# Batch 0 of a pooled-attention and feed-forward kernel: v in two loads, half its values with tokens in rows, w_in in other pieces, and batch 1 loaded as q, k, q

## The chip, the cores and the metric

The kernel runs on one core of a Trainium2 chip. The metric is the time of one execution in microseconds (us) of device time, the median of several runs. The engines are named as in the profile: PE (TensorE), DVE (VectorE), ACT (ScalarE), POOL (GpSimd) and SP (SyncE). PEld is TensorE's loading of weights.

## What is computed

Attention over pooled keys and values, and then a feed-forward layer with the gate h cos(h):

```python
k_p = k.reshape(B, H, 72, 8, 64).mean(axis=3)      # B = 8, H = 8, S = 576, D = 64
v_p = v.reshape(B, H, 72, 8, 64).mean(axis=3)
attn = softmax(q @ k_p.transpose(0, 1, 3, 2) / 8)
x = (attn @ v_p).transpose(0, 2, 1, 3).reshape(4608, 512)
h = x @ w_in                                       # 512 x 2048
out = (h * cos(h)) @ w_out                         # 2048 x 512
```

All inputs and the output are float32 in HBM. The kernel computes in bfloat16; the loads that GpSimd issues convert on the way.

## The kernel before

The 4608 tokens are cut into nine tiles of 512 (the loop over t). A tile has an up stage (x @ w_in, then cosine and product into g_sb) and a down stage (g_sb @ w_out, stored). Attention of batch b = t + 1 is fitted between the down matmuls of tile t, so batch 0's attention stands ahead of the loop and batch 1's first part (its pooling of k and the transposes of q) stands in the up stage of tile 0. From tile 1 on the down product uses seven products of half size instead of eight (down_products); tile 0 uses plain matmuls (down_mm). There is no scheduler: every engine runs its instructions in the order in which the code issues them, and that order is written out by hand.

The work is placed as follows.

- Batch 0 has four units (BY_HEADS): heads 0 to 3 with tokens 0 to 255 and 256 to 511, then heads 4 to 7 with the same tokens. For each unit there are score matmuls (`scores`, L234), an exponential on ScalarE (L241), column sums by a matmul with ones, whose inverse is taken as exp(-ln) on ScalarE (`sums_first`, L313, L317, L318), and values (`values_then`, L327), which VectorE multiplies by the inverse into xT (L329). xT holds x transposed: features in partitions, in four chunks of 128 (ki), tokens in columns. Heads 0 to 3 fill chunks 0 and 1, heads 4 to 7 chunks 2 and 3.
- v is pooled by TensorE (`pool_v_mm`, L186, head pairs j0 to j1) and copied to vz by VectorE (L188); k likewise (`pool_k_mm`, L178, copied to kk at L151). q is transposed by TensorE against an identity (`q_transpose_mm`, L215, copied at L216).
- `values_rows` (L288 to L305), used from batch 2 on, puts the tokens in rows: 8 matmuls per unit with the exponentials as weights (L296), a reciprocal (L299), one multiply (L301), and a transposing DMA into xT.
- `up_mm` (L354) issues the up matmuls of pair fp (two chunks of 128 of the 2048 hidden features), for ki from k0 to k1. `up_bank` names the PSUM bank: tile 0 takes banks 0, 2, 1 in turn. Before the loop, pairs 0 and 1 are issued for ki 0 and 1 only (L559, L560). `up_g` follows with cosine (L364) and product (L368).
- In the up stage of tile 0, the pooling of batch 1's k stands behind pair 4, and the transposes of its q behind pairs 5 and 6 (L573 to L580). The down stage of tile 0 takes w_out pieces 0, 2, 1, 3 in that order (L601), and `fill` (L617) places the attention of batch 1 between its matmuls.

Loads with conversion are issued by GpSimd in this order (L488 to L523): q heads 0 to 3 of batch 0, k heads 4 to 7, q heads 4 to 7, v; w_in pieces 0, 1 and 2 (512 columns each, all four ki chunks); k of batch 1, the first half of its q, w_in piece 3, the second half of its q; w_out piece 0, v of batch 1, and w_out pieces 2, 1 and 3. The first half of k of batch 0 comes on SyncE's queue. Some matmuls without use (`warm_up`, L528) stand ahead and between.

Of the kernel before, what the change touches and what calls it, by code (L numbers as in the profile page):

```python
# [10 lines left out]
BF16 = mybir.dt.bfloat16  # L11
# [9 lines left out]
def kernel(  # L21
# [9 lines left out]
    nc = tc.nc  # L31
# [28 lines left out]
    msb = ctx.enter_context(tc.tile_pool(name="msb", bufs=3))  # L60
    psum = ctx.enter_context(tc.tile_pool(name="psum", bufs=1, space=bass.MemoryType.PSUM))

    w_in_sb = [wpool.tile([128, KCH, 512], BF16, name=f"w_in_sb{i}") for i in range(4)]
    w_out_sb = [wpool.tile([128, 4, d_model], BF16, name=f"w_out_sb{i}") for i in range(4)]
    xT = wpool.tile([128, KCH, n_tokens], BF16, name="xT")
    g_sb = wpool.tile([128, FFCH, TILE], BF16, name="g_sb")
# [28 lines left out]
    def load_even(dst, b, src, j0=0, j1=KCH):  # L95
        nc.gpsimd.dma_start(out=dst[:, j0:j1].rearrange("p j t d -> p j (t d)"), in_=even_view(src, b, j0, j1))  # L96
# [23 lines left out]
        q_tile(b)  # L120
        load_even(staged["q", b], b, q)

    def load_w_in(cg):
        nc.gpsimd.dma_start(  # L124
            out=w_in_sb[cg],
            in_=moe_w_in[:, cg * 512:(cg + 1) * 512].rearrange("(k p) f -> p k f", p=128))


    def load_w_out(cg):
# [52 lines left out]
    def pool_v_mm(b, pair, j0=0, j1=KCH):  # L182
        vb = staged["v", b]
        for t in range(ROW):
            for hp, rows in enumerate(half):
                nc.tensor.matmul(pair[:Sp, hp, 0:(j1 - j0) * D], lhsT=groups[rows, t, :], rhs=vb[rows, j0:j1, t, :],  # L186
                                 start=(t == 0), stop=(t == ROW - 1))
        nc.vector.tensor_copy(out=v_part(b)[:, j0:j1].rearrange("p j a d -> p a j d"),  # L188
                              in_=pair[:Sp, :, 0:(j1 - j0) * D].rearrange("p a (j d) -> p a j d", d=D))
# [28 lines left out]
    def ex_col(u, i):  # L218

        (c0, n), (h0, nh) = u  # L220
        return (i // 2 % 2 * (nh // 2) + i // 4 * 2 + i % 2) * n

    def scores(b, u, pair):
        scores_mm(b, u, pair)
        scores_exp(b, u, pair)
# [59 lines left out]
        else:  # L285
            later.append(mul)

    def values_rows(b, u, pair):  # L288

        (c0, n), (h0, nh) = u  # L290
        ex = att.pop(("ex", b, u))
        ps = pair.rearrange("p b n -> p (b n)").rearrange("p (j w) -> p j w", w=2 * 128)
        for i in range(nh):
            pj, hp = divmod(i, 2)
            v_and_sum = vz[b % 2].rearrange("p j a d -> p j (a d)")[:, pj, hp * (3 * D - 1):hp * (3 * D - 1) + D + 1]
            nc.tensor.matmul(ps[0:n, pj, hp * (D + 1):(hp + 1) * (D + 1)], lhsT=ex[:, ex_col(u, i):ex_col(u, i) + n],  # L296
                             rhs=v_and_sum)
        inv = asb.tile([128, KCH, 2], FP32, name="inv_rows", tag="inv_rows", bufs=2)
        nc.vector.reciprocal(out=inv[0:n], in_=ps[0:n, :, D:D + 2])  # L299
        x = asb.tile([128, d_model], BF16, name="x_rows", tag="x_rows", bufs=4)  # L300
        nc.vector.tensor_tensor(  # L301
            out=x[0:n].rearrange("p (j a d) -> p j a d", j=KCH, a=2),
            in0=ps[0:n, :, 0:2 * (D + 2)].rearrange("p j (a w) -> p j a w", a=2)[:, :, :, 0:D],
            in1=inv[0:n].unsqueeze(3).to_broadcast([n, KCH, 2, D]), op=mybir.AluOpType.mult)
        nc.sync.dma_start_transpose(out=xT[:, :, b * S + c0:b * S + c0 + n], in_=x[0:n])  # L305

    def sums_first(b, u, cs):

        (c0, n), (h0, nh) = u
        ex = att["ex", b, u]  # L310
        for i in range(nh):
            hp = i % 2
            nc.tensor.matmul(cs[hp * 64:hp * 64 + 64, (i // 2) * n:(i // 2 + 1) * n], lhsT=ones[:Sp, :],  # L313
                             rhs=ex[:, ex_col(u, i):ex_col(u, i) + n])
        w = nh * n // 2
        inv = inverse_tile(w)
        nc.scalar.activation(out=inv, in_=cs[:, 0:w], func=ACTF.Ln)  # L317
        nc.scalar.activation(out=inv, in_=inv, func=ACTF.Exp, scale=-1.0)  # L318
        att["inv", b, u] = inv

    def values_then(b, u, ao):

        (c0, n), (h0, nh) = u
        ex = att.pop(("ex", b, u))
        for i in range(nh):
            pj, hp = divmod(h0 + i, 2)
            nc.tensor.matmul(ao[hp * 64:hp * 64 + 64, (i // 2) * n:(i // 2 + 1) * n],  # L327
                             lhsT=vz[b % 2][:, pj, 3 * hp, :], rhs=ex[:, ex_col(u, i):ex_col(u, i) + n])
        nc.vector.tensor_mul(out=x_out(b, u, slice(0, 128)), in0=cols(ao, u), in1=cols(att.pop(("inv", b, u)), u))  # L329
# [4 lines left out]
    def sin_tables():  # L334
        nc.scalar.preload_act_table_set("trig_and_small")
# [6 lines left out]
    def up_bank(t, fp):  # L342
        i = list(up_order(t)).index(fp)
        if t < FIRST:
            return (banks[0], banks[2], banks[1])[i % 3]
        return (banks[0], banks[2], banks[1], obanks)[i % 4 if i < 7 else 0]

    def up_mm(t, fp, k0=0, k1=KCH):

        h = up_bank(t, fp)  # L350
        for j in range(2):
            fc = 2 * fp + j
            for ki in range(k0, k1):
                nc.tensor.matmul(h[j] if h is obanks else h[:, j, :], lhsT=w_in_sb[fc // 4][:, ki, fc % 4:512:4],  # L354
                                 rhs=xT[:, ki, t * TILE:(t + 1) * TILE],
                                 start=(ki == 0), stop=(ki == KCH - 1))

# [130 lines left out]
    load_even(staged["q", 0], 0, q, 0, 2)  # L488
    load_even(staged["k", 0], 0, k, 2, 4)
    load_even(staged["q", 0], 0, q, 2, 4)  # L490
    load_even(staged["v", 0], 0, v)
    identity = consts.tile([128, 128], BF16, name="identity")
    make_identity(nc, identity)
    dist, sign = [x.rearrange("p f n -> p (f n)").bitcast(FP32)[:, 0:ROW * Sp].rearrange("p (t n) -> p t n", t=ROW)
# [13 lines left out]

    kv_even_tiles(1)
    q_tile(1)  # L510
    for cg in range(3):
        load_w_in(cg)
    load_even(staged["k", 1], 1, k)
    load_even(staged["q", 1], 1, q, 0, 2)
    load_w_in(3)
    load_even(staged["q", 1], 1, q, 2, 4)
    load_w_out(0)
    load_even(staged["v", 1], 1, v)
# [6 lines left out]
    def warm_up(n, bank):  # L525

        for i in range(n):
            nc.tensor.matmul(bank, lhsT=warm[:, 0:128], rhs=warm)  # L528
# [16 lines left out]
    for put in (q_transpose_mm(0, banks[2][:, 0, :], 9, 14), q_transpose_mm(0, obanks[0], 14, 18)):  # L545
        put(vec)
    sums_first(0, us[1], obanks[1])
    warm_up(2, banks[1][:, 0, :])
    scores(0, us[2], banks[0])
    scores(0, us[3], banks[2])  # L550
    pool_v_mm(0, banks[1], 0, 2)
    sums_first(0, us[2], banks[0][:, 0, :])
    values_then(0, us[0], obanks[1])
    pool_v_mm(0, banks[1], 2, 4)
    values_then(0, us[1], obanks[0])
    sums_first(0, us[3], banks[2][:, 0, :])
    values_then(0, us[2], obanks[1])
    values_then(0, us[3], banks[1][:, 0, :])
    up_mm(0, 0, 0, 2)  # L559
    up_mm(0, 1, 0, 2)  # L560
    sin_tables()

    for t in range(NT):
        b = t + 1
# [4 lines left out]
        for n, fp in enumerate(up_order(t)):  # L569
            up_mm(t, fp, 2 if n < 2 else 0)  # L570
            between = ()
            if t == 0:
                if fp == 4:  # L573
                    puts = pool_k_mm(1, obanks[0], 0, 2), pool_k_mm(1, obanks[1], 2, 4)
                elif fp in (5, 6):
                    g0 = 9 * (fp - 5)
                    puts = q_transpose_mm(1, obanks[0], g0, g0 + 5), q_transpose_mm(1, obanks[1], g0 + 5, g0 + 9)
                if fp in (4, 5, 6):
                    puts[0](vec)
                    between = ((puts[1], act),)  # L580
            up_g(t, fp, between)

            late = {5: (1,), 6: (3,)} if t == 1 else {4: (1, 2), 5: (3,)}
            sums = {} if t == 0 else late if b < B else {3: (1, 2), 4: (3,), 5: (4,)}
            put_gs(*[(i, 0) for i in sums.get(n, ())])
            if 0 < t and b < B:
                if n == 0:
                    q_transpose(b)
                    k_transpose(b)
                elif n == 2:  # L590
                    pool_rest(b, "v")
                    if b + 1 < B:
                        nc.gpsimd.tensor_copy(out=gate, in_=kk[b % 2][0:1, H - 1, 0:1])
                        load_q(b + 1)
                        load_kv(b + 1, "v", v)
            if n == 2:
                while stores:
                    stores.pop(0)()
# [16 lines left out]
            exp_tables()  # L615
            fill = [(1, lambda: scores(t, REST, banks[2])), (16, lambda: values(t, REST, banks[1]))]
        if t == 0:  # L617
            fill = [(2, lambda: scores(t, REST, banks[1])), (2, S_(0, 0)), (8, lambda: pool_v_mm(1, banks[2])),
                    (8, lambda: values(t, REST, banks[1])),
                    (8, lambda: put_weights(0, nc.vector, (3, 2))), (8, S_(1, 0)), (8, V_(0, 2)),  # L620
                    (18, S_(2, 1)), (18, lambda: put_weights(0, nc.vector, (4,))),
                    (18, lambda: put_weights(1, nc.vector, (1,))), (21, V_(1, 0, later)), (26, S_(3, 2)), (32, lambda: later.pop()()),
                    (32, V_(2, 1)), (40, V_(3, 0))]
        if t == FIRST:
            early_inverses.clear()
        if t < FIRST:
# [128 lines left out]
```

## Time and profile before

| what | value |
|---|---|
| median of 5 runs | 285.02 us (284.65 to 285.28) |
| profiled execution, its own time | 285.02 us |
| its span | 283.2 us |
| mean granted TensorE clock | 0.996 |
| TensorE busy | 275.3 us, 97% |
| VectorE, ScalarE, GpSimd busy | 213.0, 167.4 and 132.7 us |
| read from HBM, written | 36.70 MB, 9.44 MB |
| first up matmul of tile 0 | 16.75 us |
| first down matmul of tile 0 | 33.01 us |
| first up matmul of tile 1 | 53.03 us |

Times in the profile count from the start of the span. An instruction group is given by line, engine, operation, written and read tile, and count; a wait by who waited for whom. Matmuls are pipelined: a row of one shows its latency, so that its duration (379 ns for 128 x 512) is longer than the distance to the next one, and the distances are read from the starts in the timeline. The column of DMA share is the mean busy share of 16 engines, and can be over 1 where packets overlap.

### The profile page before, as it was taken

What the parts mean: (1) busy time and instruction counts of PE and PEld (TensorE: products, weight loads), DVE (VectorE), ACT (ScalarE), POOL (GpSimd) and SP (SyncE); (2) the same over time, 40 slices, a digit from 0 to 9 for tenths busy, and PEclk for the clock granted to TensorE, in tenths of its full rate; (3) what the DMA queues carried; (4) which work ended last, traced back from release to release, by engine and by line L of the source; (5) the groups of instructions that cost most, each with busy time, mean ns of one, the idle gap of its engine ahead of it and who ended that gap; (6) DMA issues with size and microseconds to landing.
All of it is one profiled execution on the core that took longest, in us unless ns stands there. A gap on an engine that the chain in (4) does not pass through costs nothing.

```text
span 283.2 us, 5887 instructions
## 1 busy us (share of the span) xinstructions
PE 275.3 (97%) x2378; PEld 185.2 (65%) x2378; DVE 213.0 (75%) x313; ACT 167.4 (59%) x199; POOL 132.7 (47%) x146
## 2 busy tenths in 40 slices
PE   7899999999999999999999999999999999999994
PEld 3555554456875687568756975688558855885683
DVE  6458768989947995699568966896689669846972
ACT  3886798368357735774567556655666555436600
POOL 8542114996599259924993389539910000000000
PEclk9999999999999999999999999999999999999998
DMA  7999999794839798997678959882660370015015
GB/s 158 194 207 210 214 204 217 130 189 65 147 48 172 126 213 136 138 178 145 107 142 144 191 80 169 147 175 52 125 148 3 58 148 19 2 27 121 2 37 112
DMA packets 56202, 36.13 MB, mean 128 GB/s; under 512 B 35440, under 2 KB 51312, under 8 KB 56176
## 3 DMA queue, kind: packets, MB, share of 16 engines
q0 software_dynamic: 18208, 18.07, 40.5%
q1 hardware_dynamic: 37328, 17.18, 29.6%
q10 hardware_dynamic: 640, 0.52, 0.8%
q8 instruction: 18, 0.29, 0.4%
q14 instruction: 8, 0.07, 0.1%
HBM read 36.70 MB, written 9.44 MB: 163 GB/s over the span
## 4 chain that ended last, share of the span: by engine, by line
PE 84%; DMA 12%; POOL 2%; issue 0%; DVE 0%; POOLq 0%
PE bank L354 34%; PE obank L432 33%; DMA w_out_sb<-in_moe_w_out_dram 7%; DMA w_in_sb<-in_moe_w_in_dram 5%; PE obank L354 5%; PE obank L371 4%; PE bank L234 3%; PE bank L296 2%; PE bank L432 2%; PE bank L269 1%; POOL q_b L96 1%; POOL w_in_sb L124 1%; POOL kv_st L96 0%; DVE o_two L448 0%; POOL identity masks.py:199 0%
## 5 line engine op out<-in xcount | busy, mean ns | idle before, releaser
L354 PE MATMUL bank<-xT,w_in_sb 128*128 128x512 bf16 x512 | 113.8, 379 | 0.1
L364 ACT ACTIVATE cos<-bank,half_pi 128x1024 f32<-128x1024 f32 x64 | 70.4, 1115 | 56.7 <-PE bank L354 55.9
L354 PEld LDWEIGHTS <-w_in_sb 128*128 128x128 bf16 x576 | 64.9, 113 | 57.3 <-issue 0.3
L368 DVE TENSOR_TENSOR g_sb<-bank,cos 128x1024 bf16<-128x1024 f32 x64 | 76.9, 1219 | 30.7 <-ACT cos L364 30.6
L157 POOL TENSOR_TENSOR half_sums<-kv_st 72x512 f32<-72x512 bf16 x48 | 54.3, 1158 | 9.1 <-DMA kv_st<-in_k_dram 8.6
L241 ACT ACTIVATE ex<-bank 72x1024 bf16<-72x1024 f32 (+1 forms) x40 | 35.0, 930 | 30.1 <-PE bank L234 30.0
L432 PEld LDWEIGHTS <-g 128*128 128x128 bf16 x512 | 47.8, 98 | 5.7
L432 PE MATMUL obank<-w,g 128*128 128x256 bf16 x368 | 42.6, 272 | 0.0
L432 PEld LDWEIGHTS <-g_sb 128*128 128x128 bf16 x384 | 37.0, 98 | 6.4
L163 POOL TENSOR_TENSOR half_sums<-half_sums 72x512 f32<-72x512 f32 x24 | 30.0, 1270 | 0.0
L432 PE MATMUL obank<-w_out_sb,g_sb 128*128 128x256 bf16 x240 | 28.9, 273 | 0.0
L398 DVE TENSOR_TENSOR g<-g_sb 128x1024 bf16<-128x1024 bf16 x32 | 21.9, 684 | 0.3
L719 POOL COPY gate<-g 1x1 bf16<-1x1 bf16 x5 | 0.9, 179 | 37.5 <-DVE inv_rows L299 37.5
L280 DVE TENSOR_TENSOR xT<-bank,inv 64x256 bf16<-64x256 f32 x14 | 5.9, 422 | 15.2 <-ACT inv L276 15.1
L301 DVE TENSOR_TENSOR x_rows<-bank,inv_rows 128x512 bf16<-128x512 f32 x24 | 16.6, 692 | 0.8
L432 PE MATMUL obank<-w_out_sb,g 128*128 128x256 bf16 x112 | 15.6, 273 | 0.0
L371 PE MATMUL obank<-w_out_sb,g_sb 128*128 128x512 bf16 x64 | 15.3, 379 | 0.3 <-DMA w_out_sb<-in_moe_w_out_dram 0.3
L432 PE MATMUL obank<-w,g_sb 128*128 128x256 bf16 x128 | 15.3, 273 | 0.0
L354 PE MATMUL obank<-xT,w_in_sb 128*128 128x512 bf16 x64 | 15.1, 379 | 0.0
L234 PE MATMUL bank<-qT,kk 64*72 64x128 bf16 (+2 forms) x288 | 12.1, 221 | 0.3 <-DVE qT L216 0.3
L332 ACT ACT_TABLE_LOAD x9 | 11.5, 1283 | 0.9 <-PEq L739 0.7
L234 PEld LDWEIGHTS <-kk 64*72 64x72 bf16 x288 | 8.7, 110 | 5.1 <-issue 3.4
(99 smaller groups left out, 270.0 us busy)
## 6 DMA issues: line engine op xcount, KB each, us to landing
out_dram<-o_two SPq DMA_DIRECT2D x64, 128.0 KB, 2.4
kv_st<-in_v_dram POOLq DMA_DIRECT2D x8, 576.0 KB, 12.3
kv_st<-in_k_dram POOLq DMA_DIRECT2D x7, 576.0 KB, 8.0
q_b<-in_q_dram POOLq DMA_DIRECT2D x6, 576.0 KB, 7.8
w_in_sb<-in_moe_w_in_dram POOLq DMA_DIRECT2D x4, 512.0 KB, 13.7
w_out_sb<-in_moe_w_out_dram POOLq DMA_DIRECT2D x4, 512.0 KB, 18.6
q_b<-in_q_dram POOLq DMA_DIRECT2D x4, 288.0 KB, 12.3
g_sb<-in_k_dram SPq DMA_DIRECT2D x1, 576.0 KB, 3.5
```

Of the source, the lines that this page charges most:

```text
L157: nc.gpsimd.tensor_tensor(out=s[:, h:h + 2], in0=x[:, h:h + 2, 0:4, :], in1=x[:, h:h + 2, 4:8, :], op=ADD)
L163: add(out=s[:, h:h + 4, 0:2, :], in0=s[:, h:h + 4, 0:2, :], in1=s[:, h:h + 4, 2:4, :], op=ADD)
L234: nc.tensor.matmul(pair[:Sp, bank, c:c + n].rearrange("p (g n) -> p g n", n=64), lhsT=kk[b % 2][half[r], key_slot(b, h0 + i, r), 0:Sp], rh ...
L241: nc.scalar.activation(out=ex[:, 0:nh * n].rearrange("p (a n) -> p a n", a=2), in_=pair[:Sp, :, 0:nh * n // 2], func=ACTF.Exp, scale=scale ...
L301: nc.vector.tensor_tensor(out=x[0:n].rearrange("p (j a d) -> p j a d", j=KCH, a=2), in0=ps[0:n, :, 0:2 * (D + 2)].rearrange("p j (a w) -> ...
L332: nc.scalar.preload_act_table_set("natural_log_exp_and_others")
L354: nc.tensor.matmul(h[j] if h is obanks else h[:, j, :], lhsT=w_in_sb[fc // 4][:, ki, fc % 4:512:4], rhs=xT[:, ki, t * TILE:(t + 1) * TILE] ...
L364: nc.scalar.activation(out=c, in_=ps, func=ACTF.Sin, bias=half_pi[:, :1])
L368: nc.vector.tensor_mul(out=o, in0=ps, in1=c)
L371: nc.tensor.matmul(o, lhsT=g_sb[:, fc, ms * 128:(ms + 1) * 128], rhs=w_out_sb[fc // 4][:, fc % 4, :], start=(fc == 0), stop=(fc == FFCH - 1))
L398: nc.vector.tensor_tensor(out=out[:, f0:f1], in0=x, in1=y, op=op)
L432: mms.append(lambda bank=bank, first=first, g=g, w=w, fc=fc, p=p: nc.tensor.matmul(bank[p], lhsT=g(fc, p), rhs=w(fc), start=(first and fc ...
```

## The change

- v of batch 0 comes in two loads, head pairs 0 and 1 and then 2 and 3.
- w_in comes in five pieces (WIN): rows 0 to 255 and rows 256 to 511 of the first 512 columns, all rows of the next 512, and rows 0 to 255 and 256 to 511 of the last 1024. All five are issued ahead of batch 1's loads, which follow as first half of q, k, second half of q.
- Batch 0's units 2 and 3 (heads 4 to 7) get their values with tokens in rows (`value_rows`, split off from `values_rows` and widened to units of 256 tokens and 4 heads), and TensorE transposes them back (`x_transpose_mm`); ScalarE copies the first into xT, VectorE the second. Their sums and inverses go.
- The order before the loop: pooling of v's first half ahead of the scores of units 2 and 3 (in the place of two warm-up matmuls), its second half behind the values of units 0 and 1. The two transposes stand between the first up matmuls, and the table of the sine is loaded ahead of those.
- In the up stage of tile 0, q's transposes stand behind pairs 4 and 6 and the pooling of k behind pair 5. The PSUM banks of tile 0's up stage are 1, 0, 2 in turn, and `fill` uses the banks accordingly.

```diff
@@ -60,7 +60,9 @@
     msb = ctx.enter_context(tc.tile_pool(name="msb", bufs=3))
     psum = ctx.enter_context(tc.tile_pool(name="psum", bufs=1, space=bass.MemoryType.PSUM))
 
-    w_in_sb = [wpool.tile([128, KCH, 512], BF16, name=f"w_in_sb{i}") for i in range(4)]
+
+    WIN = ((0, 512, 0, 2), (0, 512, 2, 4), (512, 512, 0, 4), (1024, 1024, 0, 2), (1024, 1024, 2, 4))
+    w_in_sb = [wpool.tile([128, k1 - k0, n], BF16, name=f"w_in_sb{i}") for i, (_, n, k0, k1) in enumerate(WIN)]
     w_out_sb = [wpool.tile([128, 4, d_model], BF16, name=f"w_out_sb{i}") for i in range(4)]
     xT = wpool.tile([128, KCH, n_tokens], BF16, name="xT")
     g_sb = wpool.tile([128, FFCH, TILE], BF16, name="g_sb")
@@ -120,10 +122,18 @@
         q_tile(b)
         load_even(staged["q", b], b, q)
 
-    def load_w_in(cg):
+    def load_w_in(i):
+        f0, n, k0, k1 = WIN[i]
         nc.gpsimd.dma_start(
-            out=w_in_sb[cg],
-            in_=moe_w_in[:, cg * 512:(cg + 1) * 512].rearrange("(k p) f -> p k f", p=128))
+            out=w_in_sb[i],
+            in_=moe_w_in[k0 * 128:k1 * 128, f0:f0 + n].rearrange("(k p) f -> p k f", p=128))
+
+    def w_in_part(fc, ki):
+
+        for w, (f0, n, k0, k1) in zip(w_in_sb, WIN):
+            f = fc // 4 * 512 - f0
+            if 0 <= f < n and k0 <= ki < k1:
+                return w[:, ki - k0, f + fc % 4:f + 512:4]
 
 
     def load_w_out(cg):
@@ -285,24 +295,40 @@
         else:
             later.append(mul)
 
-    def values_rows(b, u, pair):
+    def value_rows(b, u, pair):
 
         (c0, n), (h0, nh) = u
+        m = min(n, 128)
         ex = att.pop(("ex", b, u))
         ps = pair.rearrange("p b n -> p (b n)").rearrange("p (j w) -> p j w", w=2 * 128)
-        for i in range(nh):
-            pj, hp = divmod(i, 2)
-            v_and_sum = vz[b % 2].rearrange("p j a d -> p j (a d)")[:, pj, hp * (3 * D - 1):hp * (3 * D - 1) + D + 1]
-            nc.tensor.matmul(ps[0:n, pj, hp * (D + 1):(hp + 1) * (D + 1)], lhsT=ex[:, ex_col(u, i):ex_col(u, i) + n],
-                             rhs=v_and_sum)
+        for c in range(n // m):
+            for i in range(nh):
+                pj, hp = divmod(h0 + i, 2)
+                v_and_sum = vz[b % 2].rearrange("p j a d -> p j (a d)")[:, pj, hp * (3 * D - 1):hp * (3 * D - 1) + D + 1]
+                e0 = ex_col(u, i) + c * m
+                nc.tensor.matmul(ps[0:m, c * nh // 2 + i // 2, hp * (D + 1):(hp + 1) * (D + 1)],
+                                 lhsT=ex[:, e0:e0 + m], rhs=v_and_sum)
         inv = asb.tile([128, KCH, 2], FP32, name="inv_rows", tag="inv_rows", bufs=2)
-        nc.vector.reciprocal(out=inv[0:n], in_=ps[0:n, :, D:D + 2])
+        nc.vector.reciprocal(out=inv[0:m], in_=ps[0:m, :, D:D + 2])
         x = asb.tile([128, d_model], BF16, name="x_rows", tag="x_rows", bufs=4)
         nc.vector.tensor_tensor(
-            out=x[0:n].rearrange("p (j a d) -> p j a d", j=KCH, a=2),
-            in0=ps[0:n, :, 0:2 * (D + 2)].rearrange("p j (a w) -> p j a w", a=2)[:, :, :, 0:D],
-            in1=inv[0:n].unsqueeze(3).to_broadcast([n, KCH, 2, D]), op=mybir.AluOpType.mult)
-        nc.sync.dma_start_transpose(out=xT[:, :, b * S + c0:b * S + c0 + n], in_=x[0:n])
+            out=x[0:m].rearrange("p (j a d) -> p j a d", j=KCH, a=2),
+            in0=ps[0:m, :, 0:2 * (D + 2)].rearrange("p j (a w) -> p j a w", a=2)[:, :, :, 0:D],
+            in1=inv[0:m].unsqueeze(3).to_broadcast([m, KCH, 2, D]), op=mybir.AluOpType.mult)
+        return x[0:m]
+
+    def values_rows(b, u, pair):
+        (c0, n), _ = u
+        nc.sync.dma_start_transpose(out=xT[:, :, b * S + c0:b * S + c0 + n], in_=value_rows(b, u, pair))
+
+    def x_transpose_mm(b, u, x, bank):
+
+        ps = bank.bitcast(BF16)[:, 0:512].rearrange("p (j n) -> p j n", j=2)
+        for c in range(2):
+            for j in range(2):
+                nc.tensor.matmul(ps[:, j, c * 128:(c + 1) * 128], x[:, (2 * c + j) * 128:(2 * c + j + 1) * 128],
+                                 identity, is_transpose=True)
+        return lambda copy: copy(out=x_out(b, u, slice(0, 128)), in_=ps)
 
     def sums_first(b, u, cs):
 
@@ -342,16 +368,16 @@
     def up_bank(t, fp):
         i = list(up_order(t)).index(fp)
         if t < FIRST:
-            return (banks[0], banks[2], banks[1])[i % 3]
+            return (banks[1], banks[0], banks[2])[i % 3]
         return (banks[0], banks[2], banks[1], obanks)[i % 4 if i < 7 else 0]
 
-    def up_mm(t, fp, k0=0, k1=KCH):
+    def up_mm(t, fp, k0=0, k1=KCH, js=(0, 1)):
 
         h = up_bank(t, fp)
-        for j in range(2):
+        for j in js:
             fc = 2 * fp + j
             for ki in range(k0, k1):
-                nc.tensor.matmul(h[j] if h is obanks else h[:, j, :], lhsT=w_in_sb[fc // 4][:, ki, fc % 4:512:4],
+                nc.tensor.matmul(h[j] if h is obanks else h[:, j, :], lhsT=w_in_part(fc, ki),
                                  rhs=xT[:, ki, t * TILE:(t + 1) * TILE],
                                  start=(ki == 0), stop=(ki == KCH - 1))
 
@@ -488,7 +514,8 @@
     load_even(staged["q", 0], 0, q, 0, 2)
     load_even(staged["k", 0], 0, k, 2, 4)
     load_even(staged["q", 0], 0, q, 2, 4)
-    load_even(staged["v", 0], 0, v)
+    load_even(staged["v", 0], 0, v, 0, 2)
+    load_even(staged["v", 0], 0, v, 2, 4)
     identity = consts.tile([128, 128], BF16, name="identity")
     make_identity(nc, identity)
     dist, sign = [x.rearrange("p f n -> p (f n)").bitcast(FP32)[:, 0:ROW * Sp].rearrange("p (t n) -> p t n", t=ROW)
@@ -508,11 +535,10 @@
 
     kv_even_tiles(1)
     q_tile(1)
-    for cg in range(3):
-        load_w_in(cg)
+    for i in range(len(WIN)):
+        load_w_in(i)
+    load_even(staged["q", 1], 1, q, 0, 2)
     load_even(staged["k", 1], 1, k)
-    load_even(staged["q", 1], 1, q, 0, 2)
-    load_w_in(3)
     load_even(staged["q", 1], 1, q, 2, 4)
     load_w_out(0)
     load_even(staged["v", 1], 1, v)
@@ -545,20 +571,21 @@
     for put in (q_transpose_mm(0, banks[2][:, 0, :], 9, 14), q_transpose_mm(0, obanks[0], 14, 18)):
         put(vec)
     sums_first(0, us[1], obanks[1])
-    warm_up(2, banks[1][:, 0, :])
+    pool_v_mm(0, banks[1], 0, 2)
     scores(0, us[2], banks[0])
     scores(0, us[3], banks[2])
-    pool_v_mm(0, banks[1], 0, 2)
-    sums_first(0, us[2], banks[0][:, 0, :])
-    values_then(0, us[0], obanks[1])
+    values_then(0, us[0], obanks[0])
+    values_then(0, us[1], obanks[1])
     pool_v_mm(0, banks[1], 2, 4)
-    values_then(0, us[1], obanks[0])
-    sums_first(0, us[3], banks[2][:, 0, :])
-    values_then(0, us[2], obanks[1])
-    values_then(0, us[3], banks[1][:, 0, :])
+
+    x2 = value_rows(0, us[2], banks[0])
+    x3 = value_rows(0, us[3], banks[2])
+    sin_tables()
     up_mm(0, 0, 0, 2)
-    up_mm(0, 1, 0, 2)
-    sin_tables()
+    x_transpose_mm(0, us[2], x2, obanks[0])(act)
+    up_mm(0, 1, 0, 2, (0,))
+    x_transpose_mm(0, us[3], x3, obanks[1])(vec)
+    up_mm(0, 1, 0, 2, (1,))
 
     for t in range(NT):
         b = t + 1
@@ -570,10 +597,10 @@
             up_mm(t, fp, 2 if n < 2 else 0)
             between = ()
             if t == 0:
-                if fp == 4:
+                if fp == 5:
                     puts = pool_k_mm(1, obanks[0], 0, 2), pool_k_mm(1, obanks[1], 2, 4)
-                elif fp in (5, 6):
-                    g0 = 9 * (fp - 5)
+                elif fp in (4, 6):
+                    g0 = 9 * (fp - 4) // 2
                     puts = q_transpose_mm(1, obanks[0], g0, g0 + 5), q_transpose_mm(1, obanks[1], g0 + 5, g0 + 9)
                 if fp in (4, 5, 6):
                     puts[0](vec)
@@ -615,12 +642,12 @@
             exp_tables()
             fill = [(1, lambda: scores(t, REST, banks[2])), (16, lambda: values(t, REST, banks[1]))]
         if t == 0:
-            fill = [(2, lambda: scores(t, REST, banks[1])), (2, S_(0, 0)), (8, lambda: pool_v_mm(1, banks[2])),
-                    (8, lambda: values(t, REST, banks[1])),
-                    (8, lambda: put_weights(0, nc.vector, (3, 2))), (8, S_(1, 0)), (8, V_(0, 2)),
-                    (18, S_(2, 1)), (18, lambda: put_weights(0, nc.vector, (4,))),
-                    (18, lambda: put_weights(1, nc.vector, (1,))), (21, V_(1, 0, later)), (26, S_(3, 2)), (32, lambda: later.pop()()),
-                    (32, V_(2, 1)), (40, V_(3, 0))]
+            fill = [(2, lambda: scores(t, REST, banks[2])), (2, S_(0, 1)), (8, lambda: pool_v_mm(1, banks[0])),
+                    (8, lambda: values(t, REST, banks[2])),
+                    (8, lambda: put_weights(0, nc.vector, (3, 2))), (8, S_(1, 1)), (8, V_(0, 0)),
+                    (18, S_(2, 2)), (18, lambda: put_weights(0, nc.vector, (4,))),
+                    (18, lambda: put_weights(1, nc.vector, (1,))), (21, V_(1, 1, later)), (26, S_(3, 0)), (32, lambda: later.pop()()),
+                    (32, V_(2, 2)), (40, V_(3, 1))]
         if t == FIRST:
             early_inverses.clear()
         if t < FIRST:
```

## The prediction

> **What bounds the kernel now.** I read the page first, for the engine that fills the span.
>
> ```profile
> span 283.2 us, 5887 instructions
> PE 275.3 (97%) x2378; PEld 185.2 (65%) x2378; DVE 213.0 (75%) x313; ACT 167.4 (59%) x199; POOL 132.7 (47%) x146
> ```
>
> TensorE is busy almost everywhere, but the edit touches only batch 0's attention, the first w_in pieces and the loads of batch 1, all before about 43 us. So next comes the chain of waits for 0 to 60 us, in order of time (start, duration, what).
>
> ```profile
> 6.63 14.55 DMA w_in_sb<-in_moe_w_in_dram
> 21.18 0.28 issue
> 21.47 18.74 DMA w_out_sb<-in_moe_w_out_dram
> 40.20 0.04 issue
> 40.25 0.59 PE obank L371 x2
> ```
>
> The chain isn't on TensorE until 40.25: it runs back through two loads, and the later one, the third w_out piece issued, lands at 40.20. The timeline of TensorE says how close the race is (start, time, line, in brackets the idle time before).
>
> ```profile
> 13.16 0.69 PE L186 MATMUL bank<-kv_st,g 64*72 64x128 bf16 x18 [0.71 <-DMA kv_st<-in_v_dram]
> ...
> 16.75 8.83 PE L354 MATMUL bank<-xT,w_in_sb 128*128 128x512 bf16 x40
> 25.51 1.36 PE L178 MATMUL obank<-g,kv_st 64*64 64x72 bf16 x72
> ...
> 33.01 0.59 PE L371 MATMUL obank<-w_out_sb,g_sb 128*128 128x512 bf16 x2
> ...
> 38.10 1.89 PE L371 MATMUL obank<-w_out_sb,g_sb 128*128 128x512 bf16 x8
> 40.25 0.59 PE L371 MATMUL obank<-w_out_sb,g_sb 128*128 128x512 bf16 x2 [0.25 <-DMA w_out_sb<-in_moe_w_out_dram]
> ```
>
> The 40 up matmuls take (25.51 - 16.75)/40 = 0.219 us each, about 0.216 net. Eight of them from 38.10 have been issued by 38.10 + 8 x 0.216 = 39.83. TensorE could go on at 39.83 and gets its weights at 40.20: it has about 0.4 us of slack, shown as 0.25 because the last matmul drains. TensorE's earlier stall, 0.71 us on v, is therefore free today. Last, the DMA engines by stretch.
>
> ```profile
> 7.00:9.00 2.00, 1.75 (x35) 1.16 (x33) 1.09 (x3) 0.95 (x2) 2.00 (x4) 1.00 1.17 185
> 17.00:19.00 2.00, 2.00 (x11) 1.08 (x10) 0.93 (x2) 1.61 (x2) 2.00 (x5) 1.00 1.24 206
> 35.00:37.00 2.00, 1.85 (x29) 1.28 (x26) 1.26 (x3) 1.99 (x3) 0.00 (x0) 1.00 1.09 219
> ```
>
> The last two columns are DMA share and GB/s: full (over 1) and at one rate. Issue time plus time to landing gives each load's end: q's first half 6.8, k's second 8.5, q's second 10.3, v 13.1, w_in 16.05, 18.6, 21.2, then k1 (k of batch 1) 24.0, q1's first half 25.4, the fourth w_in 28.0, q1's second half 29.5, w_out 31.8, v1 34.6, w_out 37.8, 40.2, 42.7. They come one after the other, in the order of issue. So this stretch is a full pipe, and TensorE runs just behind it.
>
> **What the Trainium skill says.** "DMA: Bandwidth & Descriptors", section "Issuing engines are not separate DMA queues": all loads share the same 16 DMA engines. The trace agrees: share above 1 from 5 to 48 us. Same page, "Anatomy of one DMA": about 2 us fixed per DMA, mostly the receipt of the last write. In a full queue the trace shows none of that: w_in pieces (1 MB read) land 2.6 us apart. "TensorE: Matmul & The Clock Gate", "Back-to-back issue gap": N/2.4 + 2.5 ns, 216 ns for 512 columns; the trace's 0.216 agrees. Same page, "What's actually happening": a window of about 3.4 us without work halves the clock; the clock here is 1.00 from 3 us on, with 0.71 us the longest idle, so this trace shows no relapse.
>
> **The change part by part.**
>
> *v in two loads.* One more POOL issue, 0.78 us (L96, v). Behind it on POOL stand the identity (done at 5.2, then 6.0; the q transposes that read it start at 6.83, when q lands) and all w_in issues (5.15, then 5.95). The pipe holds q, k and v until 13.1, so both are hidden; were the pipe empty, 0.78 us would be lost. v's first half lands at 10.3 + 1.4 = 11.7 (half of v's 2.8), not 13.1.
>
> *Order ahead of the up matmuls.* The two warm-up matmuls at 11.29 and both late sums go from TensorE, and two Ln/Exp pairs (4 x 0.6 us) from ScalarE. The new order, with the old rows' durations: v at 11.75; 18 pooling matmuls, copy to vz 0.8 us after their start (13.16 to 13.95), 12.55 to 12.97; meanwhile scores (0.63) 12.3 to 12.95, exps to 14.75 behind the Ln/Exp that ends at 12.85; values of unit 0 at 13.05, its multiply 0.52 us later (14.43 to 14.95), 13.6; the next starts 0.63 later; then, behind both on VectorE, the second vz copy, 14.86 to 15.27. Token-row values need that copy: TensorE idles about 1.1 us from 14.2 to 15.33. L296's 8 matmuls go out in 0.25 us; VectorE then does reciprocal 0.20 and multiply 0.69 twice (L299, L301; starts about 0.85 apart): 15.8 to 17.6. TensorE meanwhile runs 6 up matmuls and one set of transposes. The second set at 17.65, its copy (0.41, begun 0.4 later) to 18.46. Up matmuls on rows 256 to 511 start at **F = 18.5**. Before: 16.75 + 8 x 0.216 = 18.48. So removing some 2.4 us of ScalarE work and the v stall buys nothing at F: the vz copy, two multiplies and a round trip through transposes are late next. The moved, renamed activation table load (1.28) stays beside other work: ScalarE is free from 14.75, first needed near 17.2.
> F has bounds: 17.9 if the two vz-dependent waits overlap, 19.4 if each of the five TensorE-VectorE-TensorE handoffs costs 0.2 more (L327's wait for vz).
>
> *w_in pieces and batch 1's order.* Same bytes. Before, the loads from v's end to the fourth w_in piece are w_in x4, k1, q1's first half; after, the same set, with k1 last. So **k1 lands where the fourth w_in piece did, 28.0**. w_in is complete earlier, at 28.0 less k1 (2.8) and q1 (1.4) = 23.8; the fifth pair's matmuls that need it come at F + 26 x 0.216 = 24.1. Two loads more (v, w_in's first) stand in the pipe: between nothing and 0.35 each (288 KB early took 1.7, twice that less v's 2.8 is 0.6; but q1's took 1.4, which leaves 0). Rows of 1024 columns may go at w_out's 216 GB/s against 206: 1.05 MB gains at most 0.25. I take both together at +0.05. Eight loads are in flight at most (the twelfth, a w_out piece, is issued when v, the fourth, has landed; it becomes the fourteenth, behind a half of w_in), always several us ahead: nothing.
>
> *q, k, q in the up stage.* F + 32 x 0.216 = 25.4 for five pairs, transposes 0.5 (q1 there at 25.1), sixth pair 1.73: 27.65, and now k must be there: 28.0, a **new stall of 0.35**. Then pooling of k 1.29, pair 1.73, transposes 0.5, pair 1.73: the down stage at 33.25, not 33.01. Its kk copies on VectorE (4 x 0.31) and ScalarE end near 30.5, the scores that read them begin near 33.8.
>
> *Banks renamed, two helpers split.* The same instructions for t > 0; in the down stage of tile 0 each user takes the bank that its predecessor's counterpart left. Nothing.
>
> **Sum.** From 33.25 to the third w_out piece the old 6.82 us (39.83 - 33.01) give 40.07; the same bytes stand ahead of that piece, so it lands at 40.2 + 0.05. The later of the two decides: 40.25, before 40.20. As two nearly equal arms meet, the expected maximum lies slightly above: +0.1. All after it is TensorE work that doesn't change. The next w_out piece (42.7, wanted at 42.86) moves alike. Profiled execution: 285.02 us (span 283.2, 1.8 around it), equal to the median of the runs; **285.1**.
>
> **The rivals.**
> *Transfers that cost* (slower): its place is the pipe before 28 us. For it: the small early loads ran at 185 GB/s, and 1.7 us for 288 KB is 0.3 worse than half of v. If each added load costs 0.35 to 0.45, third w_out and k1 land 0.7 to 0.9 later, and the kernel goes to **285.85**. It decides from 0.57 us in sum. Against: q1's halves took 1.4 and 1.5.
> *A late front* (slower too): F at 19.4 makes the sixth pair end at 28.55, 0.55 behind k1; less the 0.15 of slack, 285.5, just inside; with a halved clock after the idle at 14.2 it is more.
> *The front pays* (faster): F at 17.9 would give 284.4 if nothing but TensorE decided. For it: TensorE is 97% busy. Against: k1 at 28.0 and w_out at 40.2 stop it; only a pipe 0.6 faster lets it through, while the larger rows give 0.25 at most.
> *Nothing at all, since the loads rule:* that is my forecast.
>
> **How the numbers follow.** This kernel can be told from no change beyond about 0.2%, 0.57 us. Pipe rules, time stays: 0.70, own range 284.7 to 285.5. Costly transfers 0.13 and late front with or without clock 0.06: slower 0.19. Front pays through a faster pipe: 0.11. The range takes in 284.5 (rows at 216 GB/s, and 0.25 of spread among the runs) up to 285.9 (the rival's 285.85); what lies beyond each end is under one in ten.
>
> **What would show it.** In the profile after: v's first pooling near 11.8; TensorE idle near 14.2 to 15.3; F near 18.5; a wait of the pooling matmuls of batch 1's k for their load, 0.2 to 0.5 us, near 28; the down stage near 33.25; a wait for w_out that ends at 40.1 to 40.4. The forecast is wrong if the third w_out piece lands beyond 39.7 to 40.8, or if TensorE isn't waiting for it and arrives later than 40.8; or if anything after 43 us changes its length.

## The result and the profile after

| | before | after |
|---|---|---|
| median | 285.03 us (80 runs) | 285.76 us (43 runs, 285.10 to 287.18) |
| ratio | 1 | 1.0027 (95% interval 1.0019 to 1.0034) |
| profiled execution: time, span | 285.02, 283.2 us | 286.09, 284.0 us |
| time less span, median of the runs | 1.79 us (1.77 in one comparison) | 2.13 us |
| span, median of the runs | 283.3 us in two comparisons, 283.6 in a third | 283.6 us |

The changed kernel is slower by 0.73 us. The range that was given, 284.5 to 285.9, holds it; the likeliest case, no change within 0.2%, does not. Roughly half of the loss is inside the span and half (2.13 - 1.79 = 0.34 us) isn't in the trace at all.

The page of the changed kernel, in the two lines that were shown of before:

```profile
span 284.0 us, 5903 instructions
PE 275.8 (97%) x2384; PEld 185.5 (65%) x2384; DVE 212.1 (75%) x316; ACT 165.5 (58%) x196; POOL 133.4 (47%) x148
```

TensorE's busy time rose by 0.5 us, the span by 0.8. The chain of waits for 0 to 60 us of the changed kernel (start, duration, what), with most of its pieces left out:

```profile
1.42 6.91 DMA q_b<-in_q_dram
8.33 0.05 issue
...
14.27 1.92 ACT ex L251 x2
16.19 0.65 PE bank L309 x16
...
18.96 0.43 DVE xT L331
19.39 0.14 issue
19.53 7.11 PE bank L380 x32
...
39.33 2.16 PE obank L397 x10
```

No load of w_in or w_out is left in it. It starts with q's first half, which lands at 8.33 here (6.8 in the profile of before), runs through ScalarE's exponentials and the row values to VectorE's copy of the second transposed unit (L331), and from 19.53 on it is TensorE's own work. The timeline of TensorE in the same kernel:

```profile
16.18 0.65 PE L309 MATMUL bank<-vz,ex 72*128 72x65 bf16 x16 [0.94 <-ACT ex L251]
...
19.53 7.11 PE L380 MATMUL bank<-xT,w_in_sb 128*128 128x512 bf16 x32 [0.18 <-DVE xT L331]
...
28.80 1.36 PE L188 MATMUL obank<-g,kv_st 64*64 64x72 bf16 x72
...
34.07 0.59 PE L397 MATMUL obank<-w_out_sb,g_sb 128*128 128x512 bf16 x2
...
39.17 2.32 PE L397 MATMUL obank<-w_out_sb,g_sb 128*128 128x512 bf16 x10
```

F, the start of the up matmuls on rows 256 to 511, is 19.53 (forecast 18.5, bounds 17.9 to 19.4). The down stage starts at 34.07, and the ten matmuls from 39.17 run on without a wait: eight of them belong to the second w_out piece and end at 39.17 + 8 x 0.216 = 40.9, and the third w_out piece landed at 40.1. That wait, the last word in the kernel before, is gone, and TensorE is 0.65 us later at tile 1 (53.68 against 53.03). The DMA engines are as full as before (last two columns, share and GB/s):

```profile
7.00:9.00 2.00, 1.47 (x18) 0.75 (x13) 1.35 (x5) 0.00 (x0) 1.32 (x3) 1.00 1.19 197
17.00:19.00 2.00, 1.99 (x16) 0.83 (x14) 1.47 (x4) 1.06 (x2) 2.00 (x3) 1.00 1.17 213
35.00:37.00 2.00, 1.85 (x16) 0.92 (x14) 1.58 (x2) 1.97 (x3) 0.00 (x0) 1.00 1.06 215
```

### The profile page after: what moved, and what is told of

The parts are those of the page before. It is cut to its first block, busy times and chain, and to the rows that moved or that the text cites. A ratio compares the mean times of both kernels' runs of the same rounds, so it can differ in the third digit from the quotient of the medians.

```text
span 284.0 us, 5903 instructions
## 1 busy us (share of the span) xinstructions
PE 275.8 (97%) x2384; PEld 185.5 (65%) x2384; DVE 212.1 (75%) x316; ACT 165.5 (58%) x196; POOL 133.4 (47%) x148
## 4 chain that ended last, share of the span: by engine, by line
PE 92%; DMA 2%; ACT 2%; DVE 1%; issue 1%; POOL 0%; POOLq 0%; DVEq 0%
PE bank L380 39%; PE obank L458 33%; PE obank L380 5%; PE obank L397 4%; PE bank L244 3%; DMA q_b<-in_q_dram 2%; PE bank L309 2%; PE bank L458 2%; PE bank L279 1%; ACT ex L251 1%; PE obank L188 0%; DVE g_sb L394 0%; PE obank L225 0%; PE bank L196 0%; ACT cos L390 0%
## 5 line engine op out<-in xcount | busy, mean ns | idle before, releaser
L314 DVE TENSOR_TENSOR x_rows<-bank,inv_rows 128x512 bf16<-128x512 f32 x26 | 18.0, 692 | 0.9
```

What stands on the lines that cost most here:

```text
L314: nc.vector.tensor_tensor(out=x[0:m].rearrange("p (j a d) -> p j a d", j=KCH, a=2), in0=ps[0:m, :, 0:2 * (D + 2)].rearrange("p j (a w) -> ...
```

## The experiments

**Both kernels once more.** One profile is one execution; these two ask what differs between executions.

> The kernel before once more, for a second profile. Theory 1 (late front): the landing of q's first half and the start of the up matmuls on rows 256 to 511 (F) differ from execution to execution by about 1 us, and this kernel hides it behind the wait for w_out, so its span is 283.0 to 283.6 us whatever F is. Theory 2 (the second load of v delays q's first half): q's first half lands near 6.8 us again.

> The changed kernel once more, for a second profile. Theory 1: the span is F + 264.5 us, within 0.2, as in the first profile (19.53 and 284.0), and no wait for w_out is left. Theory 2: q's first half lands near 8.3 us again, and F is near 19.5.

The kernel before in its second profile, on TensorE:

```profile
8.06 0.45 PE L215 MATMUL bank<-identity,q_b 128*128 128x128 bf16 x5 [0.74 <-DMA q_b<-in_q_dram]
...
17.55 8.83 PE L354 MATMUL bank<-xT,w_in_sb 128*128 128x512 bf16 x40
...
38.91 2.35 PE L371 MATMUL obank<-w_out_sb,g_sb 128*128 128x512 bf16 x10
```

q's first half landed at 8.0 in the unchanged kernel, and F is 17.55 + 1.73 = 19.28. In the changed kernel's second profile it landed at 6.9, and F is 18.52, the 18.5 of the forecast. So the second load of v doesn't delay q; the landing differs from execution to execution in both kernels (over all profiles of this document 6.8 to 8.0 with one load of v, 6.8 to 8.3 with two), and F follows it. The span of before_again, 283.7, lies 0.1 beyond what Theory 1 allowed. The trace has 16 completion marks for a load: in the changed kernel's first profile 14 of them come by 6.5, one at 7.3 and one at 8.3; in the kernel before all 16 between 5.7 and 6.8. There one or two stragglers make the load late; in before_again five marks come after 7.0. What holds them up isn't known.

The changed kernel's second profile also ends later than F says (283.6, against F + 264.5 = 283.0):

```profile
18.52 7.41 PE L380 MATMUL bank<-xT,w_in_sb 128*128 128x512 bf16 x32 [0.18 <-DVE xT L331]
25.77 0.67 PE L225 MATMUL obank<-identity,q_b 128*128 128x128 bf16 x9
26.27 1.89 PE L380 MATMUL bank<-xT,w_in_sb 128*128 128x512 bf16 x8
28.23 1.36 PE L188 MATMUL obank<-g,kv_st 64*64 64x72 bf16 x72
```

32 up matmuls take 25.77 - 18.52 = 7.25 us, not 6.91 (w_in's last piece landed at 24.4, wanted at 24.1), and pooling starts at 28.23, where the pair ahead of it was issued by 26.27 + 1.73 = 28.0: k1 landed at 28.2. Together this is 0.44 us ahead of tile 1; another 0.20 us is lost inside tile 1, which is taken up below. So the late front alone (Theory 1) is not enough.

**The change in two.** The loads without the front, and the front without the loads.

```diff
 loads_alone: before, with
+    v in two loads; WIN, w_in_part; w_in x5, q1 first half, k1, q1 second half
+    pool_k_mm behind pair 5, q_transpose_mm behind pairs 4 and 6
 front_alone: after, with
-    WIN, w_in_part; w_in x5, q, k, q
+    w_in 0, 1, 2; k1; q1 first half; w_in 3; q1 second half (up stage k, q, q)
```

> The front of the kernel before, with all the loads of the changed one (v in two, w_in in five pieces, q, k, q and the order of the up stage that goes with it). Theory 1: the wait for w_out at about 40.2 still sets the end, 284.9 to 285.2 us, ratio 1.000. Theory 2 or dear loads: q's first half late, w_out late, 285.6 us or more.

> The changed kernel's front and v in two loads, with the old w_in pieces and the old order of batch 1's loads. Theory 1: the front is as late as in the changed kernel, 285.6 to 285.9 us, ratio 1.0025. If the order of the loads is the cause (k of batch 1 late, or w_in), 285.0 us.

Loads alone: 286.16 us, 1.0038 (1.0023 to 1.0053). Front alone: 285.79 us, 1.0018 (1.0004 to 1.0032); before was 285.35 on that chip. (The ratios are those on record, from the fast runs; they are not quotients of the medians.) Theory 1 falls: the loads alone cost, with the old front. TensorE shows where, in loads_alone:

```profile
26.52 1.89 PE L363 MATMUL bank<-xT,w_in_sb 128*128 128x512 bf16 x8
29.14 1.36 PE L187 MATMUL obank<-g,kv_st 64*64 64x72 bf16 x72 [0.73 <-DMA kv_st<-in_k_dram]
```

It waits 0.73 us for k1, which landed at 29.1. In front_alone the wait is elsewhere:

```profile
17.27 1.05 PE L371 MATMUL bank<-xT,w_in_sb 128*128 128x512 bf16 x4 [1.00 <-DMA w_in_sb<-in_moe_w_in_dram]
```

The first w_in piece, whole, landed at 17.2 there, and F is 19.72. The changed kernel, with half pieces, has no such wait.

**k1 earlier, k1 later, v's copy earlier, and both.** Four kernels that tell the two arms, F and k1, apart.

```diff
 k_early:  w_in's last 1024 columns as two pieces of 512 columns, all rows;
-    w_in x5, q1 first half, k1, q1 second half
+    w_in x4, q1 first half, k1, last w_in, q1 second half
 k_late:
-    w_in x5, q1 first half, k1, q1 second half
+    w_in x5, q1 first half, q1 second half, k1
 v_early:
+    pool_v_mm(0, banks[1], 2, 4)
     values_then(0, us[0], obanks[0])
     values_then(0, us[1], obanks[1])
-    pool_v_mm(0, banks[1], 2, 4)
 k_v_early: k_early and v_early
```

> The changed kernel, but w_in's last 1024 columns come as two pieces of 512 columns, with all rows, and q1's first half and k1 are loaded between them (order: w_in, q, k, last w_in piece, q). Theory K (k of batch 1 lands last and is passed on to the end, landing + 12.2 us against the third w_out piece): k1 lands near 25.5 instead of 28.1 to 28.4, TensorE doesn't wait for it, and the kernel is 0.3 to 0.5 us faster than the changed one, 1.000 to 1.001 of before. Theory F (the late front alone): no gain, 1.0025.

> The changed kernel with k1 loaded after both halves of q1, 288 KB or 1.4 us later. Theory K: TensorE waits for k1 at about 29.6 to 30.5, and the kernel is 1.0 to 1.4 us slower than the changed one, ratio to before 1.006 to 1.0075. Theory F: the end is set by the front, 0.5 us of the delay at most shows, ratio below 1.0045.

> The changed kernel with the pooling of v's second half, and its copy to vz, ahead of the values of units 0 and 1. The copy no longer stands behind two multiplies on VectorE, so F falls by 0.4 to 0.6 us (18.0 to 19.0). Theory F: the kernel is 0.3 to 0.5 us faster than the changed one. Theory K: nothing, since TensorE waits that much longer for k1; ratio to before 1.002 to 1.003.

> Both edits: k1 ahead of the last w_in piece, and v's second half pooled early. Both theories: neither k1 nor the front is the last arm, the third w_out piece (landing 40.0 to 40.8) sets the end again; 0.999 to 1.000 of before. If it is slower than that, something else in the change costs.

| kernel | median us | ratio to before | median span |
|---|---|---|---|
| k_early | 285.90 | 1.0030 (1.0017 to 1.0044) | 283.75 |
| k_late | 286.69 | 1.0063 (1.0051 to 1.0075) | 284.60 |
| v_early | 285.64 | 1.0023 (1.0013 to 1.0033) | 283.50 |
| k_v_early | 285.42 | 1.0015 (1.0001 to 1.0028) | 283.30 |

k_late shows k1 as a full arm: 1.4 us of waiting in its waits of TensorE, and a median 0.93 us above the changed kernel.

```profile
PE obank L188 <- DMA kv_st<-in_k_dram: 1.4, 1, 1.4
```

k_early missed its forecast: without any wait for k1 it isn't faster than the changed kernel. Its own profile, with a span of 283.4, is one of its shorter executions, so which arm holds the others isn't shown. v_early missed in part: F comes 3.02 us behind the end of ScalarE's exponentials (15.44 to 18.46) where after_again has 3.35 (15.17 to 18.52), a gain of 0.3 and not 0.4 to 0.6, and the time gains nothing that can be told from zero. So taking away one arm alone doesn't win the time back. The intervals of k_early, v_early and k_v_early overlap, so their medians alone don't show an order, and the argument rests on the profiles. Both edits together have the median span of before, 283.3, in the same comparison, and the wait for w_out is back (k_v_early, TensorE):

```profile
40.06 0.59 PE L397 MATMUL obank<-w_out_sb,g_sb 128*128 128x512 bf16 x2 [0.21 <-DMA w_out_sb<-in_moe_w_out_dram]
...
70.21 0.41 PE L244 MATMUL bank<-qT,kk 64*72 64x128 bf16 x8 [0.55 <-DVE g_sb L394]
```

The time of k_v_early is nonetheless 285.42, as time outside the span is 2.13 us in it too. The second line is taken up below.

**Time outside the span.** It is narrow within each kernel (1.72 to 1.85 before, 2.07 to 2.18 after) and shifts in steps: one more load from GpSimd's queue in front_alone, 1.92; two more in loads_alone and the four above, 2.09 to 2.13.

```diff
 more_loads: before, in load_q (batches 2 to 7)
-    load_even(staged["q", b], b, q)
+    load_even(staged["q", b], b, q, 0, 2)
+    load_even(staged["q", b], b, q, 2, 4)
 q1_whole: before
-    load_even(staged["q", 1], 1, q, 0, 2)
-    load_w_in(3)
-    load_even(staged["q", 1], 1, q, 2, 4)
+    load_even(staged["q", 1], 1, q)
+    load_w_in(3)
 more_stores: before, in rows_out, tiles 1 to 3: each store as two of half the columns
 v_split_alone: before
-    load_even(staged["v", 0], 0, v)
+    load_even(staged["v", 0], 0, v, 0, 2)
+    load_even(staged["v", 0], 0, v, 2, 4)
```

> The kernel before, with the q load of batches 2 to 7 as two loads of half the heads: six more loads that GpSimd issues, all after 28 us and off the path. Theory O (each load that GpSimd issues adds about 0.15 us outside the span: 1.79 before, 1.92 with one more, 2.13 with two more): the time outside the span is 2.6 to 2.9 us, the span 283.2 to 283.7, the time 285.9 to 286.4. Rival (the 0.34 us come from where or what the changed loads are, or from its other instructions): outside stays at 1.8, time 285.0 to 285.3.

> The kernel before with q of batch 1 as one load, ahead of the last w_in piece: one load fewer. Theory O: outside the span 1.62 to 1.66 us. Inside, q1 lands near 26.8 and the last w_in piece near 28.1 to 29.4, where the seventh pair wants it at 29.05: the third w_out piece still sets the end, so the span stays at 283.2 to 283.4. Time 284.8 to 285.0, ratio 0.9993 to 1.0. Rival: outside 1.79, ratio 1.0 to 1.001.

> The kernel before with the stores of tiles 1 to 3 in two halves of the columns: 24 more DMAs issued by SyncE. If every DMA costs time outside the span, outside is 5 us or more; if only those of GpSimd's queue do, it stays at 1.8.

> The kernel before with v of batch 0 in two loads and nothing else. Theory O: outside the span 1.93, span as before (283.2 to 283.6), since the third w_out piece sets it; ratio 1.0004 to 1.001. Rival (the second load also costs in the pipe ahead of k and w_out): span 0.3 us longer as well, ratio 1.0015 or more.

| kernel | GpSimd's loads | outside us | median span | ratio |
|---|---|---|---|---|
| q1_whole | -1 | 1.79 | 283.6 | 1.0009 (0.9994 to 1.0023) |
| before | 0 | 1.79 | 283.3 | 1 |
| more_stores | 0 (24 more on SyncE) | 1.79 | 287.9 (one run) | |
| v_split_alone | +1 | 1.90 | 283.3 | 1.0007 (0.9991 to 1.0022) |
| after | +2 | 2.13 | 283.6 | 1.0027 |
| more_loads | +6 | 2.41 | 283.3 | 1.0017 (1.0002 to 1.0031) |

GpSimd's loads cost outside the span wherever they stand (those of more_loads are issued after 28 us and leave the span alone); SyncE's stores don't. But it isn't 0.15 us for each: six give 0.62, two 0.34, one 0.11, and one fewer gives nothing, against the forecast. What in these loads does it stays open, and for the stores there is one run. The long span of more_stores is another matter: VectorE waits 3.18 us for earlier stores before it can write the store buffer (o_two), and TensorE 2.21 us behind it, at 105 us. The span of q1_whole missed its forecast too (283.6, for 283.2 to 283.4); the next section has the reasons. v_split_alone has the span of before, so v's second load isn't dear in the pipe.

## Why the prediction was right, and where it was wrong

The range held, but the reasons behind its ends did not. Its upper end, 285.9, was set for costly transfers, which didn't come; the loss has two other sources, one of them outside the trace. That it fell inside is in part luck. Two of the forecast's own signs of being wrong came true: in the first profile TensorE doesn't wait for the third w_out piece and arrives at 40.9, later than 40.8, and in the second something after 43 us changes its length.

Three arms, chains of work that all have to be through, meet ahead of tile 1, whose first up matmul starts when the last of them is through. The front comes through at F + 34.15 (from the changed kernel, 53.68 - 19.53), the third w_out piece at its landing + 12.83 (from before, 53.03 - 40.20), and k1 at its landing + 24.93 (from k_late, 54.20 - 29.27). With the order of before, where k is pooled one pair and one set of transposes earlier, k1's constant is 27.19 (from before_again, 53.45 - 26.31, and 0.05 from landing to pooling). A landing here is the last completion mark of the load. With these constants the other profiles are told to 0.03 us:

| kernel | F | front | k1 | k1's arm | w_out | w_out's arm | latest | seen |
|---|---|---|---|---|---|---|---|---|
| before_again | 19.28 | 53.43 | 24.66 | 51.85 | 40.63 | 53.46 | 53.46 | 53.45 |
| after_again | 18.52 | 52.67 | 28.19 | 53.12 | 39.86 | 52.69 | 53.12 | 53.11 |
| loads_alone | 19.09 | 53.24 | 29.10 | 54.03 | 40.74 | 53.57 | 54.03 | 54.02 |
| front_alone | 19.72 | 53.87 | 25.09 | 52.28 | 40.71 | 53.54 | 53.87 | 53.90 |
| k_early | 18.86 | 53.01 | 26.05 | 50.98 | 40.26 | 53.09 | 53.09 | 53.09 |
| v_early | 18.46 | 52.61 | 28.43 | 53.36 | 40.07 | 52.90 | 53.36 | 53.35 |
| k_v_early | 18.21 | 52.36 | 25.65 | 50.58 | 40.02 | 52.85 | 52.85 | 52.84 |
| v_split_alone | 18.93 | 53.08 | 23.86 | 51.05 | 39.48 | 52.31 | 53.08 | 53.08 |

The profiles of more_loads and more_stores fit as well. Only q1_whole doesn't (52.54, seen 52.83): its last w_in piece lands at 29.19, and the seventh pair waits for it from 28.97 to 29.23.

- *The pipe and its order* were right: k1 landed at 28.2 and 28.4 in the changed kernel where 28.0 was forecast, and the rival of dear transfers falls, with the third w_out piece at 39.9 and 40.1, earlier than the 40.25 of the sum.
- *F = 18.5* was right for an execution whose q lands at 6.9. The mistake was to take the landing of one profile as fixed: at 8.3 F is 19.53, beyond the late front's 19.4. The reason given for the idle time ahead of the token-row values was only half right: the trace puts it down to ScalarE's exponentials, which end 0.05 us behind the copy to vz in both profiles (16.18 against 16.13, and 15.17 against 15.12). The forecast had them done half a us ahead of it. That is why v_early, which moves the copy, gains less than it was to.
- *"The later of the two decides: 40.25"* is the step of the sum that failed, as a size. TensorE's arm at the third w_out piece was put at 40.07; it was 28.23 + 5.27 + 6.83 = 40.33 in after_again (0.2 of the difference from k1's landing) and 40.9 in the first profile, while the piece it was set against came 0.2 to 0.4 early. So it isn't two equal arms: the loads' arm fell behind and k1's or F's leads by 0.4 to 0.8. The forecast also gave each a single value; a maximum over three arms that jitter by about 1 us each lies higher than the maximum of their middles, and the change had moved k1's arm up from between 51 and 52 to the other two.
- *"1.8 around it"* failed outright: time around the span was carried over as a constant, and it rose by 0.34 us, nearly half of the loss.
- *q, k, q* and its new stall were forecast at 0.35 and seen at 0.2 (after_again) to 0.73 (loads_alone) where F was early enough.
- *The clock* was read from its column alone. That column is 1.00 throughout, but the first 512-column matmuls start 0.427 us apart, up to 4.4 us in the kernel before and up to 5.3 in the changed one, and 0.216 apart later: they begin at half the rate. The forecast's "no relapse" holds, as the up matmuls are 0.216 apart.
- *"All after it is TensorE work that doesn't change"* failed as well. Tile 1 takes 28.83 us in the kernel before and in the changed kernel's first profile, but 29.03 in its second, 29.36 in q1_whole and 29.66 in k_v_early. VectorE, in k_v_early:

```profile
65.70 1.59 DVE L424 TENSOR_TENSOR g<-g_sb 128x1024 bf16<-128x1024 bf16 x1
67.21 1.21 DVE L394 TENSOR_TENSOR g_sb<-bank,cos 128x1024 bf16<-128x1024 f32 x1
68.35 0.68 DVE L424 TENSOR_TENSOR g<-g_sb 128x1024 bf16<-128x1024 bf16 x1
```

The first takes 1.59 us where the same operation takes 0.68. GpSimd runs beside it, in the same kernel:

```profile
47.35 4.93 POOL L167 TENSOR_TENSOR half_sums<-kv_st 72x512 f32<-72x512 bf16 x4 [9.66 <-DMA kv_st<-in_k_dram]
...
65.48 1.26 POOL L179 TENSOR_TENSOR vz<-half_sums 72x512 bf16<-72x512 f32 x1
```

The Trainium skill, "SBUF — State Buffer", section "Who interferes with whom", says that a VectorE instruction with two SBUF inputs and a GpSimd instruction that reads SBUF exclude each other, and the later one waits for the whole of the earlier. The trace agrees: VectorE's operation is over 0.55 us after GpSimd's ends at 66.74. It holds up the product that frees a bank, hence the 0.55 us at 70.21. The same is seen in q1_whole, which has the old front:

```profile
65.15 1.27 POOL L169 TENSOR_TENSOR vz<-half_sums 72x512 bf16<-72x512 f32 x1
65.68 1.30 DVE L398 TENSOR_TENSOR g<-g_sb 128x1024 bf16<-128x1024 bf16 x1
69.90 0.41 PE L234 MATMUL bank<-qT,kk 64*72 64x128 bf16 x8 [0.34 <-DVE g_sb L368]
```

What sets GpSimd's operation is one more load. GpSimd waits for k of batch 2 (the 9.66 us above) and then works through without a break of more than 0.3 us, so that the operation ends 19.0 to 19.5 us after that landing in every profile of this document. Tile 2 begins 15.76 us after that end (k_v_early, 82.50 - 66.74), or 28.83 us after tile 1 began, whichever is later. This tells tile 2's start in all fourteen profiles to 0.01 us; five of them:

| kernel | k of batch 2 lands | GpSimd's end | + 15.76 | tile 1 + 28.83 | tile 2 seen |
|---|---|---|---|---|---|
| before | 46.51 | 66.03 | 81.79 | 81.86 | 81.86 |
| after | 46.34 | 65.88 | 81.64 | 82.51 | 82.51 |
| after_again | 46.85 | 66.38 | 82.14 | 81.94 | 82.14 |
| q1_whole | 46.91 | 66.42 | 82.18 | 81.66 | 82.19 |
| more_loads | 46.57 | 66.10 | 81.86 | 81.63 | 81.86 |

So in the profile that the forecast was made from, a further arm was through only 0.07 us before TensorE, and shows as no wait (in before_again it was 0.6 us, as this landing differs from execution to execution too). An earlier TensorE walks into it: in more_loads tile 1 starts 0.23 us earlier than in before, and tile 2 starts at the same time. With all three arms ahead of tile 1 out of the way, that execution could have gained no more than 0.07 us, so the rival of a front that pays, 284.4, left this arm out. This arm also made 0.20 us of the loss in the changed kernel's second profile.

No version of the changed kernel beat the kernel before. The nearest, k_v_early, has its median span and pays for its two loads outside of it.

## What to carry to other kernels

Where several arms meet within a few tenths of a us, cost each to the same point, with its spread over executions, and expect the maximum to lie above the latest middle; a second profile of the unchanged kernel costs little and shows which landing jitters. Moving a load behind another in a full pipe moves no bytes, but it makes a new last arm of the load moved back. An arm that shows as no wait can stand within 0.1 us of the one that does, so ask what a gain would meet next. Before cutting a load in two, look at the time outside the span as well as at the span.

## What the runs showed of the hardware that was not expected

- Loads that GpSimd issues lengthen the execution outside the traced span: 1.79 us to 1.90 or 1.92 with one more, 2.09 to 2.13 with two, 2.41 with six; 24 more stores from SyncE leave 1.79 (one run).
- A load of 288 KB at the start landed between 6.8 and 8.3 us in two profiles each of the two kernels, at no lower rate (185 GB/s from 7 to 9 us where it came at 6.8, 197 where it came at 8.3), as one to five of its 16 completion marks come up to 1.8 us behind the rest, and part of the lag stays for the loads behind it (1.2 us at q and 0.65 us at v between the two profiles of the kernel before).
- k_early and v_early each work on one arm and changed nothing that can be told from zero against the changed kernel; with both the median span is that of before, though the intervals overlap.
- A VectorE operation with two SBUF inputs, 0.68 us alone, that starts beside GpSimd's is over 0.55 to 0.56 us after GpSimd's end in four profiles (after_again, more_loads, q1_whole, k_v_early), so that it takes 0.96 to 1.59 us.
